# A residual load moved ahead of the FFN's operand loads, a q load moved to an earlier step, and a v store cut in four, in a fused attention and FFN kernel

## The chip, the cores and the metric

The kernel runs on one core of a Trainium2 chip. The metric is the time of one execution on the device in microseconds (us), the median of three runs.

## The reference

One prompt of S = 2048 tokens with D = 576 channels passes a block in three parts: a layer norm modulated by a condition c, an attention with a compressive memory, and a SwiGLU feed-forward network (FFN) with FF = 4608. Cut to what matters:

```
q, k, v = heads(h @ wq), heads(h @ wk), heads(h @ wv)   # 32 heads of 18, 4 segments of 512 tokens
phi = lambda t: where(t > 0, t + 1, exp(t))
for each segment:
    a_loc = softmax(q k^T * scale + mask) v
    a_mem = phi(q) M / (phi(q) z)
    a = sigmoid(beta) * a_mem + (1 - sigmoid(beta)) * a_loc
    M, z = M + phi(k)^T v, z + sum(phi(k))
x1 = x + gate_a * (a @ wo)                              # the residual
h2 = layernorm(x1), modulated
out = x1 + gate_b * ((silu(h2 @ w_gate) * (h2 @ w_up)) @ w_down)
```

h is the modulated layer norm of x. Everything is float32 in and out.

## The kernel before

The order of the instructions on each engine is the order in which the code emits them. Matrix products in float32 are made of parts: an operand is split into a rounded high half and a low half, and three or more matmuls take the place of one.

The span has four stages. Up to 230 us come layer norm and projections; `vproj` (line 593) makes v of one segment, and its results of segment 3 go from the SBUF tile `vs[3]` to `vD[3]` in device memory in one store by ScalarE's queue (line 608). From 230 to 578 us come the attention units, 32 of them: unit u is one segment and a group of heads. Each unit runs through 11 steps, and a table `PAT` (line 66) lists for each step the events that are woven into it; row 1 is that of the second and the fourth of a segment's eight groups. Event "f" loads phi(q)'s input `qF` for the next unit into the tile `qf` (`phi_q`, line 874), and ScalarE's `phi_q2` (events "g", lines 883 to 885) and PoolE's `phi_q3` ("h", line 892) work on it. `put_m` (line 195, line 198 in the trace) writes the maximum of the scores, `mr`, into the tile `qs`; "U" and "V" load k and q of a later unit. `wo_m` and `wo_x` (lines 823 and 837) are the output projection of the segment before: `wo_m` the matmuls, `wo_x` the sum with the residual input `xr` (line 840) and the store of the sum to `xD` (line 842). `load_xr` (line 799) loads `xr` from the input; each tile of 128 tokens of a segment has one, and the buffers are reused by the segment after.

From 578 to 597 us the output projection of segment 3 runs by itself, while the operands of the FFN's first block are loaded: `load_o` loads the tile `O` of gate and up weights (512 KB), `load_y` one of seven activation operands `y` (1024 + 192 KB), `load_r` small weight parts `wr`, `load_d` the down weights `dr`. From 597 us on comes the FFN: `step` (line 1348) runs one of seven products of a block by `prod` (line 1308, matmuls of line 1315). The first products run in the order 1, 6, 2, 7, 5, 4; product 2 takes y operand 1, product 7 operand 5, product 5 operand 3, and the operands of 6 and 4 (and 3) are made on the chip. ScalarE copies a product's bank (`cu`, `tb`, `tc`, line 1344) and casts weights to their high half `wh` (line 1276), VectorE makes the low half `wl` (line 1277) and sums of `O` (line 1265), PoolE other sums of `O` (line 1270) and of `dr` (lines 1291, 1298). `store_o` (line 1253) stores the sums of `O` to `oD` on ScalarE's queue.

Two more things set the order. DMAs go out on SyncE's and ScalarE's queues, each in order. Each DMA takes one of eight semaphores in turn, and its queue first waits until the last DMA with the same semaphore has landed. So a DMA can wait for a much earlier one of the other queue.

In the setup of the FFN (about line 1520), tiles 0 to 2 of `xr` of segment 3 are loaded first, and tile 3 only after `load_d`, because its buffer still holds segment 2's tile 3. That tile isn't stored by `wo_x` (the exception in line 841) but by a store right ahead of this load (line 1531).

Of the kernel before, what the change touches and what calls it, by code (L numbers as in the profile page):

```python
# [15 lines left out]
P = 128  # L16
S = 2048
D = 576
# [45 lines left out]
E2 = 1  # L64
BK = 0
PAT = (["E", "", "m U D", "c", "n V G", "Q d", "M0", "g M1 M2 M3 X", "h A0", "R S q T Y Z B0", "A1 f P z B1 C"],
# [3 lines left out]
LNA = 1  # L70
# [8 lines left out]
def f32(ap):  # L79
    return ap.bitcast(F32)  # L80
# [3 lines left out]
def block(ctx: ExitStack, tc: tile.TileContext, x, wqk, wv, wo, beta, wgu, wgr, wd, c, crow, w_mod, w_mod0, w_mod1, w_modc, xt, out):  # L84
    nc = tc.nc
# [7 lines left out]
    def chain(*g):  # L93
        for a in g:
            yield from a

    def once(g):
        yield next(g)
# [5 lines left out]
    def mm14(ps, wh, wl, xh, xl, xr, wstat):  # L104
        k = 0
        for kt in range(5):
            if kt < 4:
                pairs = [(wh(kt), xh(kt)), (wl(kt), xh(kt)), (wh(kt), xl(kt))]
            else:
                pairs = [(wh(4), xr()), (wl(4), xr())]  # L110
            for w, a in pairs:
                a, b = (w, a) if wstat else (a, w)
                nc.tensor.matmul(ps, lhsT=a, rhs=b, start=(k == 0), stop=(k == 13))  # L113
                k += 1
# [49 lines left out]
    vD = [dr.tile([P, 4, VC], F32, tag=f"vD{s}", name=f"vD{s}") for s in range(NSEG)]  # L164
# [3 lines left out]
    xD = [dr.tile([P, 4, D], F32, tag=f"xD{s}", name=f"xD{s}") for s in range(NSEG)]  # L168
# [105 lines left out]
    with ExitStack() as p1:  # L274
# [70 lines left out]
        with ExitStack() as p0:  # L345
# [41 lines left out]
            for b in range(3):  # L387
                n = P if b < 2 else 64
# [174 lines left out]
        def proj(s, t):  # L563
            hh, hl, hr = hT[s]
            pp = first.pop(t, None) if s == 0 else None
            if pp is None:
                pp = ps.tile([P, L], F32, tag="p", name="pp", bufs=3)
                mm14(pp, lambda k: wqkh[:, t, k, :], lambda k: wqkl[:, t, k, :], lambda k: hh[k],
                     lambda k: hl[k], lambda: hr, True)
            f = pb.tile([P, L], F32, tag="pf", name="pf")  # L570
            fb = pb.tile([P, 2, L], F32R, tag="fh", name="fh", bufs=3)
            fh, fl = fb[:, 0], fb[:, 1]
            if t < 5:
                nc.scalar.copy(f, pp)
            nc.scalar.copy(fh, pp)
            nc.vector.tensor_tensor(fl, pp, f32(fh), op=ALU.subtract)
            if s > 0 and t >= 5:
                nc.scalar.copy(f, pp)
            k0, k1 = 128 * t, min(128 * t + 128, D)
            if k0 < D:  # L580
                nc.sync.dma_start(kD[s][k0:k1], f32(fb[:k1 - k0]))
            q0, q1 = max(128 * t - D, 0), 128 * t + 128 - D
            if q1 > 0:
                r = P - q1 + q0
                nc.sync.dma_start(qD[s][q0:q1, 0:2], f32(fb[r:]))
                nc.sync.dma_start(qD[s][q0:q1, 2], f32(fh[r:]))
                if s > 0:
                    nc.sync.dma_start(qF[s][q0:q1, :], f[r:])
            return f

        vs = {}

        def vproj(s, i):
            hh, hl, hr = hT[s]
            if i == 0:
                vs[s] = w1.tile([P, 4, VC], F32, tag="vs", name=f"vs{s}", bufs=2)
                nc.gpsimd.memset(vs[s][:, :, :H * VW].rearrange("p i (a b) -> p i a b", b=VW)[:, :, :, DH:], 1.0)
                nc.gpsimd.memset(vs[s][:, :, H * VW:], 0.0)
            for h in range(2):
                pv = ps.tile([P, L], F32, tag="p", name="pv", bufs=3)  # L600
                sl = slice(288 * h, 288 * h + 288)
                tk = slice(128 * i, 128 * i + 128)
                mm14(pv[:, :288], lambda k: wvh[:, k, sl], lambda k: wvl[:, k, sl], lambda k: hh[k][:, tk],
                     lambda k: hl[k][:, tk], lambda: hr[:, tk], False)
                o = vs[s][:, i, 304 * h:304 * h + 304].rearrange("p (a b) -> p a b", b=VW)
                nc.scalar.copy(o[:, :, :DH], pv[:, :288].rearrange("p (a b) -> p a b", b=DH))
            if i == 3:
                nc.scalar.dma_start(vD[s], vs[s])

        for t in range(1, 4):  # L610
# [16 lines left out]
        for s in range(NSEG):  # L627
            if s == 0:
                gp, gw = prep(1), load_wv()
                g = chain(once(gp), once(gw), once(gp), once(gw), once(gp), gw, gp)  # L630
            else:
                g = prep(s + 1) if s + 1 < NSEG else iter(())
# [6 lines left out]
            for t in QKORD:  # L639
# [4 lines left out]
                f = proj(s, t)  # L644
# [13 lines left out]
            for i in range(4):  # L658
                if i == 3:
                    run(g)  # L660
                vproj(s, i)
                next(g, None)
                next(g, None)
                if s > 0:
                    for _ in range(E2):
                        next(ge, None)
                    next(gl, None)
# [117 lines left out]
    oT, orr, pto = {}, {}, {}  # L785
# [13 lines left out]
    def load_xr(s, i):  # L799
        xr = o3.tile([P, D], F32, tag="xr", name="xr") if s < 3 or i in (0, 3) else xp.tile([P, D], F32, tag="xs", name="xr")  # L800
        r = L * s + P * i
        nc.sync.dma_start(xr, x[r:r + P, :])
        return xr
# [33 lines left out]
    def wo_x(s, i, h):  # L837
        xr = oT[s, i][2]
        sl = slice(288 * h, 288 * h + 288)
        nc.vector.tensor_tensor(xr[:, sl], wps[0][:, :288], xr[:, sl], op=ALU.add)  # L840
        if h == 1 and (s, i) != (2, 3):
            nc.sync.dma_start(xD[s][:, i, :], xr)

    lnv = {}
# [389 lines left out]
    def load_y(t, o):  # L1234
        nc.sync.dma_start(f32(y[:, o, 0:4]), yD[t][o][:, 0:4])
        nc.sync.dma_start(f32(y[0:96, o, 4]), yD[t][o][0:96, 4])
# [8 lines left out]
    def load_o(t, p, z):  # L1245
        O[p, z] = o = opl.tile([P, 7, 2, P], F32, tag="O", name="O", bufs=2)
        if t == 0:
            nc.sync.dma_start(o[:, 0:4], wgu[p, z])
        else:
            nc.sync.dma_start(o[:, 0:3], wgu[p, z][:, 0:3])  # L1250
            nc.sync.dma_start(o[:, 3:7], oD[p][z])
# [4 lines left out]
    def load_r(p, z):  # L1256
        b, g = divmod(2 * p + z, 4)
        for i in range(3):
            nc.sync.dma_start(f32(R[z][32 * i:32 * i + 32]), rD[b][i % 2][32 * g:32 * g + 32])
# [20 lines left out]
    def load_d(t, p):  # L1280
        RW[p] = r = rp.tile([P, 7, 288], F32, tag="d", name="dr_")
        if t == 0:
            for f in range(2):
                nc.sync.dma_start(r[:, 2 * f:2 * f + 2].rearrange("p a b -> p (a b)"), wd[2 * p + f])
        else:
            nc.sync.dma_start(r[:, :NS[p]], wdD[p][:, :NS[p]])
# [157 lines left out]
    def plain(t, p, c):  # L1444
        pd = new_dn("pd", c)
        b, h, c = c // 4, c // 2 % 2, c % 2
        for i in range(2):
            tk = slice(128 * (2 * c + i), 128 * (2 * c + i) + 128)
            k = 0
            for f in range(2):  # L1450
                ah, al = AP[p % 2, (f, b)]
                dh, dl = DP[p % 2, (f, h)]
                for a, w in ((ah, dh), (ah, dl), (al, dh)):
                    nc.tensor.matmul(pd[:, i, :288], lhsT=a[:, tk], rhs=w, start=(k == 0), stop=(k == 5))  # L1454
                    k += 1
        d = x11[t] if b and h else acc[2 + h + 2 * b]
        o = d[:, 2 * c:2 * c + 2]
        nc.vector.tensor_tensor(o, o, pd[:, :, :288], op=ALU.add)
        if p == NPR - 1:
            if t:  # L1460
                store(t, b, h, d, c)
            elif c == 1:
                return lambda: store(t, b, h, d)
# [9 lines left out]
    with tc.manual_schedule():  # L1473
# [7 lines left out]
        for u in range(NU + 1):  # L1481
            s, q = divmod(u, 8)
# [35 lines left out]
        xr3 = {i: load_xr(3, i) for i in range(3)}  # L1518
# [5 lines left out]
        load_y(0, 0)  # L1524
        load_o(0, 0, 1)
        load_r(0, 0)
        load_y(0, 1)
        load_y(0, 5)
        load_y(0, 3)
        load_d(0, 0)  # L1530
        nc.sync.dma_start(xD[2][:, 3, :], oT[2, 3][2])
        xr3[3] = load_xr(3, 3)
        load_r(0, 1)
        wo_r(3, 0)
        wo_z(3)
# [9 lines left out]
        for i in range(4):  # L1545
            for h in range(2):
                for c in range(WC):
                    n = 8 * i + 4 * h + c
# [34 lines left out]
        n, nw = 0, PF  # L1583
# [5 lines left out]
        for t in range(2):  # L1589
            for p in range(NPR):  # L1590
# [18 lines left out]
                for k in range(14):  # L1609
                    z, m = ZM[k]  # L1610
# [59 lines left out]
                    if prev is not None and is_plain(*prev):  # L1670
# [3 lines left out]
                        if (CHE if t == 0 else CHB if p == 0 else CH0)[k]:  # L1674
                            f = plain(*prev, chunk)
# [123 lines left out]
```

## Time and profile before

| | us |
|---|---|
| median of 3 runs | 1837.87 (1834.95 to 1840.02) |
| profiled execution | 1840.8 |
| its span | 1839.0 |
| PE busy | 1797.0 |
| DVE busy | 1486.7 |
| ACT busy | 1086.2 |
| POOL busy | 675.4 |

PE is TensorE, DVE VectorE, ACT ScalarE, POOL GpSimd, SP SyncE; a q behind a name (SPq) is the engine's sequencer, which issues DMAs. Times are from the start of the span. Rows of the timeline give the start, the duration, engine, line, operation and tile (out<-in), and in brackets the idle time of the engine ahead of the instruction and what ended it. Rows of waits give who waited for whom, the total, the number of times and the longest. Rows of the chain give the pieces of the path that ends last. Rows of windows give the stretch, its length, the busy time and number of instructions of PE, weight load, DVE, ACT and POOL, the granted clock of TensorE, the busy share of the DMA engines and GB/s.

### The profile page before, as it was taken

What the parts mean: (1) busy time and instruction counts of PE and PEld (TensorE: products, weight loads), DVE (VectorE), ACT (ScalarE), POOL (GpSimd) and SP (SyncE); (2) the same over time, 40 slices, a digit from 0 to 9 for tenths busy, and PEclk for the clock granted to TensorE, in tenths of its full rate; (3) what the DMA queues carried; (4) which work ended last, traced back from release to release, by engine and by line L of the source; (5) the groups of instructions that cost most, each with busy time, mean ns of one, the idle gap of its engine ahead of it and who ended that gap; (6) DMA issues with size and microseconds to landing.
All of it is one profiled execution on the core that took longest, in us unless ns stands there. A gap on an engine that the chain in (4) does not pass through costs nothing.

```text
span 1839.0 us, 31444 instructions
## 1 busy us (share of the span) xinstructions
PE 1797.0 (98%) x10627; PEld 1525.5 (83%) x10627; DVE 1486.7 (81%) x3371; ACT 1086.2 (59%) x2371; POOL 675.4 (37%) x1104
## 2 busy tenths in 40 slices
PE   7999999999999799999999999999999999999999
PEld 5888866777777688888888888898888888888888
DVE  7556387888885599898889899868888888888886
ACT  4333287878776467777777777634454544544541
POOL 3444067775566375665665665400000000000000
PEclk9999999999999899999999999999999999999999
DMA  7768765667656745445555444484433333334331
GB/s 275 258 220 285 247 200 176 213 196 224 173 165 183 242 133 191 156 156 177 157 156 185 139 135 168 149 292 165 128 106 89 117 106 113 102 97 128 106 102 52
DMA packets 146003, 306.26 MB, mean 167 GB/s; under 512 B 30932, under 2 KB 61780, under 8 KB 143924
## 3 DMA queue, kind: packets, MB, share of 16 engines
q1 hardware_dynamic: 135092, 260.19, 45.7%
q10 hardware_dynamic: 10752, 44.07, 6.1%
q8 instruction: 85, 1.39, 0.3%
q14 instruction: 74, 0.61, 0.1%
HBM read 198.69 MB, written 104.94 MB: 165 GB/s over the span
## 4 chain that ended last, share of the span: by engine, by line
PE 91%; DMA 3%; ACT 2%; DVE 2%; issue 1%; SPq 1%; POOL 0%; ACTq 0%; DVEq 0%; POOLq 0%
PE A L1315 25%; PE pd L1434 19%; PE C L1315 13%; PE B L1315 6%; PE pp L113 6%; PE av L725 4%; PE s L210 4%; PE pv L113 3%; PE s L701 3%; PE pd L1454 3%; PE pw L835 3%; ACT Pt L708 1%; PE pn L903 1%; DMA xD<-xr 1%; DMA qf<-qF 1%
## 5 line engine op out<-in xcount | busy, mean ns | idle before, releaser
L1315 PE MATMUL A<-y,wh 128*128 128x512 f32 x1152 | 405.2, 392 | 11.8 <-ACT tb L1344 11.1
L1442 DVE TENSOR_TENSOR acc<-acc,pd 128x576 f32<-128x576 f32 x327 | 245.0, 750 | 79.2 <-PE pd L1434 73.1
L215 DVE CUSTOM_DVE_ANT_0 junk<-s,tri 128x256 bf16<-128x256 f32 (+3 forms) x512 | 221.4, 484 | 63.2 <-PE s L210 50.0
L1434 PE MATMUL pd<-dh,ah 128*128 128x288 f32 x896 | 267.3, 298 | 0.0
L1434 PE MATMUL pd<-dl,ah 128*128 128x288 f32 x896 | 263.7, 294 | 0.0
L1434 PE MATMUL pd<-dh,al 128*128 128x288 f32 x896 | 262.4, 293 | 0.0
L1315 PEld LDWEIGHTS A<-y,wh 128*128 128x128 f32 x1152 | 216.8, 188 | 51.0 <-ACT tb L1344 11.5
L1277 DVE TENSOR_TENSOR wl<-O,wh 128x256 fp32r<-128x256 f32 x504 | 238.8, 477 | 1.4 <-ACT wh L1276 0.7
L1315 PE MATMUL A<-y,wl 128*128 128x512 f32 x576 | 225.1, 391 | 0.0
L708 ACT ACTIVATE Pt<-s 128x512 f32<-128x512 f32 (+1 forms) x352 | 182.7, 558 | 46.0 <-PE s L701 28.9
L1276 ACT CAST wh<-O 128x256 fp32r<-128x256 f32 x504 | 198.3, 406 | 13.9 <-DVE xr L840 12.4
L1315 PE MATMUL C<-y,wh 128*128 128x512 f32 x576 | 203.4, 394 | 0.0
L1434 PEld LDWEIGHTS pd<-dh,ah 128*128 128x128 f32 x896 | 168.1, 188 | 18.7 <-ACT pd L1410 4.0
L1270 POOL TENSOR_TENSOR O<-O 128x128 f32<-128x128 f32 x280 | 155.0, 587 | 76.2 <-DMA O<-in_wgu_dram 35.0
L1434 PEld LDWEIGHTS pd<-dl,ah 128*128 128x128 f32 x896 | 169.5, 189 | 16.2
L1380 DVE TENSOR_TENSOR al<-sg,ah 128x512 fp32r<-128x512 f32 x240 | 176.6, 736 | 6.7 <-ACT ah L1379 6.5
L1434 PEld LDWEIGHTS pd<-dh,al 128*128 128x128 f32 x896 | 169.0, 189 | 0.0
L1379 ACT CAST ah<-sg 128x512 fp32r<-128x512 f32 x240 | 149.0, 621 | 24.3 <-DVE sg L1339 23.7
L701 PE MATMUL s<-qs,ks 110*128 110x512 f32 (+2 forms) x384 | 143.7, 392 | 6.8 <-ACT Pt L708 4.6
L210 PE MATMUL s<-ks,qs 108*128 108x256 f32 (+3 forms) x512 | 144.1, 335 | 2.6 <-DVE mx L215 2.2
L1315 PEld LDWEIGHTS C<-y,wh 128*128 128x128 f32 x576 | 108.6, 189 | 19.0
L1315 PEld LDWEIGHTS A<-y,wl 128*128 128x128 f32 x576 | 108.5, 188 | 14.9
(389 smaller groups left out, 4077.5 us busy)
## 6 DMA issues: line engine op xcount, KB each, us to landing
wr<-rD SPq DMA_DIRECT2D x216, 112.0 KB
O<-in_wgu_dram SPq DMA_DIRECT2D x36, 512.0 KB
oD<-O ACTq DMA_DIRECT2D x36, 512.0 KB
O<-oD SPq DMA_DIRECT2D x36, 512.0 KB
ks<-kD SPq DMA_DIRECT2D x96, 144.0 KB
O<-in_wgu_dram SPq DMA_DIRECT2D x36, 384.0 KB
qs<-qD SPq DMA_DIRECT2D x64, 192.0 KB
y<-yD SPq DMA_DIRECT2D x11, 1024.0 KB
```

Source lines behind the costliest of these rows:

```text
L113: nc.tensor.matmul(ps, lhsT=a, rhs=b, start=(k == 0), stop=(k == 13))
L210: nc.tensor.matmul(bank[:, n * (h - h0):n * (h - h0) + n], lhsT=qst[b][0:108, h, 128 * i:128 * i + 128], rhs=kst[b][0:108, h // 2, 0:n], s ...
L215: nc.vector.tensor_tensor_reduce(junk[:, :n], bank[:, n * (h - h0):n * (h - h0) + n], tri[:, L - n:], 1.0, -3e38, op0=ALU.add, op1=ALU.max ...
L701: nc.tensor.matmul(bank[:, n * (g - h):n * (g - h + w)].rearrange("p (a b) -> p a b", a=w), lhsT=kst[u % NB][0:110, g // 2, 128 * j:128 * ...
L708: nc.scalar.activation(pt[:, h:h + per, :n], bank[:, :n * per].rearrange("p (a b) -> p a b", a=per), AF.Exp, scale=SCALE)
L1270: eng.tensor_tensor(o[:, d, i, s_], o[:, a, i, s_], o[:, b, i, s_], op=op)
L1276: nc.scalar.copy(wh, o)
L1277: later.append(lambda: nc.vector.tensor_tensor(wl, o, f32(wh), op=ALU.subtract))
L1315: nc.tensor.matmul(bank, lhsT=a, rhs=b, start=(first and n == 0), stop=(n == 6), skip_group_check=not first)
L1380: later.append(lambda: nc.vector.tensor_tensor(al, src, f32(ah), op=ALU.subtract))
L1434: nc.tensor.matmul(pd[:, i, :288], lhsT=a[:, tk], rhs=w, start=(add and k == 0), stop=(k == 2), skip_group_check=not add)
L1442: nc.vector.tensor_tensor(o, o, pd[:, :, :288], op=ALU.add)
```

## The change

Four edits in three parts. The first part: `wo_x` stores every tile to `xD`, tile 3 of segment 2 too, and the load of segment 3's tile 3 stands right behind `load_r(0, 0)`, ahead of the y loads. The second: event "f" stands in step 1 of row 1 of the table and not in step 7, for six units. The third: in segment 3 each of four token tiles of v is stored by itself once it is made.

```
-       ["U E D", "", "Q l m", "", "M0 M1 M2 M3 X G p n V A0 B0", "", "A1 q c x B1", "f d", "", "", "C g Y h P"],
+       ["U E D", "f", "Q l m", "", "M0 M1 M2 M3 X G p n V A0 B0", "", "A1 q c x B1", "d", "", "", "C g Y h P"],
...
-            if i == 3:
+            if s == 3:
+                nc.scalar.dma_start(vD[s][:, i], vs[s][:, i])
+            elif i == 3:
                 nc.scalar.dma_start(vD[s], vs[s])
...
         nc.vector.tensor_tensor(xr[:, sl], wps[0][:, :288], xr[:, sl], op=ALU.add)
-        if h == 1 and (s, i) != (2, 3):
+        if h == 1:
             nc.sync.dma_start(xD[s][:, i, :], xr)
...
         load_r(0, 0)
+        xr3[3] = load_xr(3, 3)
         load_y(0, 1)
         load_y(0, 5)
         load_y(0, 3)
         load_d(0, 0)
-        nc.sync.dma_start(xD[2][:, 3, :], oT[2, 3][2])
-        xr3[3] = load_xr(3, 3)
         load_r(0, 1)
```

Lines behind the second edit are 2 higher in the kernel after (842 becomes 844), those behind the last 1 higher. The order of TensorE, VectorE and PoolE stays as it is.

SyncE's queue where attention ends, before (rows of DMAs, out<-in, with the shape; y<-yD_123 is operand 5, yD_121 operand 3):

```order
L1259 DMA wr<-rD_0_198 32x896
L1235 DMA y<-yD_119 128x2048
L1236 DMA y<-yD_119 96x512
L1235 DMA y<-yD_123 128x2048
L1236 DMA y<-yD_123 96x512
L1235 DMA y<-yD_121 128x2048
L1236 DMA y<-yD_121 96x512
L1284 DMA dr__8588<-in_wd_dram 128x576 x2
L1531 DMA xD_142<-xr 128x576
L802 DMA xr<-in_x_dram 128x576
L1259 DMA wr<-rD_0_198 32x896
```

The same stretch of SyncE's queue after the change:

```order
L1261 DMA wr<-rD_0_198 32x896
L804 DMA xr<-in_x_dram 128x576
L1237 DMA y<-yD_119 128x2048
L1238 DMA y<-yD_119 96x512
L1237 DMA y<-yD_123 128x2048
L1238 DMA y<-yD_123 96x512
L1237 DMA y<-yD_121 128x2048
L1238 DMA y<-yD_121 96x512
L1286 DMA dr__8594<-in_wd_dram 128x576 x2
L1261 DMA wr<-rD_0_198 32x896
```

The load passes seven DMAs; its store has left this stretch and stands some ten rows further up, behind the last store to `xh` and ahead of the loads of the three other `xr` tiles.

SyncE's queue in an odd unit, before (`mr` is the maximum of the scores):

```order
L187 DMA ks_80<-kD_106 36x2x512 x3
L198 DMA qs_87<-mr 1x16x128 x2
L193 DMA qs_79<-qD_102 48x2x512 x2
L193 DMA qs_79<-qD_102 6x2x512 x2
L1137 DMA rD_0_198<-yh_2509 128x896
L1138 DMA rD_1_199<-yh_2509 128x896
L1128 DMA yh_2509<-in_wgr_dram 128x512
L877 DMA qf<-qF_111 126x512
L992 DMA woraw<-in_wo_dram 128x576
```

The same after:

```order
L187 DMA ks_80<-kD_106 36x2x512 x3
L879 DMA qf<-qF_111 126x512
L198 DMA qs_87<-mr 1x16x128 x2
L193 DMA qs_79<-qD_102 48x2x512 x2
L193 DMA qs_79<-qD_102 6x2x512 x2
L1139 DMA rD_0_198<-yh_2512 128x896
L1140 DMA rD_1_199<-yh_2512 128x896
L1130 DMA yh_2512<-in_wgr_dram 128x512
L994 DMA woraw<-in_wo_dram 128x576
```

The load of `qf` passes the copies into `qs` and three DMAs of another job.

ScalarE at the end of `vproj` of segment 3, before:

```order
L606 COPY vs_2342<-pv 128x16x18 x3
L336 COPY gbB<-pc 128x288 x2
L606 COPY vs_2342<-pv 128x16x18 x4
L608 DMA vD_117<-vs_2342 128x2496
L708 ACTIVATE Pt<-s_2540 128x512
```

And after:

```order
L606 COPY vs_2342<-pv 128x16x18
L608 DMA vD_117<-vs_2342 128x624
L606 COPY vs_2342<-pv 128x16x18 x2
L608 DMA vD_117<-vs_2342 128x624
L336 COPY gbB<-pc 128x288 x2
L606 COPY vs_2342<-pv 128x16x18 x2
L608 DMA vD_117<-vs_2342 128x624
L606 COPY vs_2342<-pv 128x16x18 x2
L608 DMA vD_117<-vs_2342 128x624
L710 ACTIVATE Pt<-s_2543 128x512
```

Four quarter stores stand between the copies in place of one store behind the last.

More of the change, by code (lines that the diff above doesn't have):

```diff
@@ L606, in vproj @@
                 nc.scalar.copy(o[:, :, :DH], pv[:, :288].rearrange("p (a b) -> p a b", b=DH))
-            if i == 3:
+            if s == 3:
+                nc.scalar.dma_start(vD[s][:, i], vs[s][:, i])
+            elif i == 3:
                 nc.scalar.dma_start(vD[s], vs[s])
@@ L840, in wo_x @@
         nc.vector.tensor_tensor(xr[:, sl], wps[0][:, :288], xr[:, sl], op=ALU.add)
-        if h == 1 and (s, i) != (2, 3):
+        if h == 1:
             nc.sync.dma_start(xD[s][:, i, :], xr)
@@ L1526, in block @@
         load_r(0, 0)
+        xr3[3] = load_xr(3, 3)
         load_y(0, 1)
@@ L1530, in block @@
         load_d(0, 0)
-        nc.sync.dma_start(xD[2][:, 3, :], oT[2, 3][2])
-        xr3[3] = load_xr(3, 3)
         load_r(0, 1)
```

2 rows, old and new, of the table PAT are left out of this document.

## The prediction

> **What bounds the kernel now.** I read the summed chain first, then the chain piece by piece round the point where attention ends, then the engines' own rows there.
>
> ```profile
> PE 91%; DMA 3%; ACT 2%; DVE 2%; issue 1%; SPq 1%; POOL 0%; ACTq 0%; DVEq 0%; POOLq 0%
> ```
>
> TensorE carries 91% of the chain, so an edit that leaves its work alone can win only where it idles on the chain. The 3% of DMA is mostly in one place:
>
> ```profile
> 571.80 0.45 DVE xr L840
> ...
> 590.05 3.74 PE pw L835 x28
> ...
> 593.81 0.46 DVE xr L840
> 594.27 0.22 DVE O L1265
> 594.49 11.22 DMA xD<-xr
> ...
> 605.73 3.37 DMA xr<-in_x_dram
> ...
> 609.22 0.46 DVE xr L840
> ...
> 611.66 0.38 DVE xr L840
> ...
> 612.06 0.40 ACT wh L1276
> ...
> 614.35 3.35 PE A L1315 x7
> ```
>
> Last on the chain are a 288 KB store of a residual tile of segment 2, which takes 11.22 us, and the load into the same buffer, 3.37 us. VectorE stands at the sum that needs this load (line 840, tile 3 of segment 3), ScalarE behind VectorE, TensorE behind ScalarE. TensorE's rows, with the idle time before an instruction in brackets:
>
> ```profile
> 601.48 0.39 PE L1315 MATMUL B<-y,wh 128*128 128x512 f32 x1
> ...
> 602.84 0.39 PE L1315 MATMUL B<-y,wr 128*128 128x512 f32 x1
> 614.35 0.79 PE L1315 MATMUL A<-y,wh 128*128 128x512 f32 x1 [11.12 <-ACT tb L1344]
> 614.94 0.63 PE L1315 MATMUL A<-y,wl 128*128 128x512 f32 x1
> ...
> 620.05 0.40 PE L1315 MATMUL A<-y,wh 128*128 128x512 f32 x1
> ```
>
> Six steps from 601.48 to 602.84 are 0.227 us a matmul. Without the wait product 7 would begin at 602.84 + 0.23 = 603.07, product 5 seven matmuls later at 604.66, product 4 at 606.25. Product 4 began at 620.05. So the wait costs **13.8 us**: 11.1 of idling and 2.5 to 2.7 of slow matmuls after it (14 take 5.70 us where 3.18 would do). The windows (busy us of each engine, then granted clock, share of the DMA engines, GB/s) show the same:
>
> ```profile
> 560.00:580.00 20.00, 16.85 (x140) 12.10 (x141) 7.68 (x18) 13.15 (x29) 10.77 (x17) 1.00 0.39 124
> 580.00:600.00 20.00, 19.32 (x143) 18.61 (x142) 12.40 (x23) 9.09 (x19) 13.89 (x18) 1.00 1.00 286
> 600.00:610.00 10.00, 3.23 (x14) 2.31 (x13) 0.78 (x3) 0.00 (x0) 5.59 (x13) 0.79 0.68 203
> 610.00:615.00 5.00, 0.65 (x2) 0.56 (x3) 4.94 (x12) 2.92 (x8) 1.04 (x2) 0.50 1.05 404
> 615.00:620.00 5.00, 5.00 (x14) 3.94 (x13) 1.34 (x3) 3.03 (x5) 1.39 (x4) 0.55 0.94 292
> 620.00:640.00 20.00, 20.00 (x97) 16.92 (x97) 16.52 (x31) 11.80 (x29) 8.14 (x15) 1.00 0.57 192
> ```
>
> The clock is 0.50 to 0.55 after the idle stretch and 1.00 from 620, with TensorE full: time won ahead of 620 is kept. The Trainium skill ("TensorE: Matmul & The Clock Gate", What's actually happening) says that an idle window of about 3.4 us halves the clock and about 3.4 us of work restores it; by that rule a wait that shrinks below it costs its idling alone, and the rows here agree, with 0.63 us a matmul at 614.94 against 0.40 at 620.05.
>
> **The change part by part.** *Store and load of the residual tile.* SyncE's rows (start, then issue time with its blocking):
>
> ```profile
> 574.07 1.35 SPq L802 DMA_DIRECT2D xr<-in_x_dram  x3
> ...
> 579.16 2.59 SPq L1259 DMA_DIRECT2D wr<-rD  x3
> 581.79 0.55 SPq L1235 DMA_DIRECT2D y<-yD  x1
> ...
> 589.92 0.34 SPq L1235 DMA_DIRECT2D y<-yD  x1
> ...
> 613.50 0.33 SPq L1248 DMA_DIRECT2D O<-in_wgu_dram  x1
> ```
>
> The store's data is ready at 571.80 + 0.45 = 572.25, so in the new place SyncE issues it at about 574.0, while the queue is nearly empty (124 GB/s was the mean of the 20 us before 580); it lands long before the load is issued behind the three wr loads, at 579.16 + 2.59 plus the store's 0.35, about **582.2**. What was issued from 574.1 to 581.8 (three xr loads, two of O, a y operand of 1.2 MB, wr) is 3.4 MB, 12 us at the window's 286 GB/s, so until 588 from about 576 on; with the store and the load itself, 0.59 MB or 2.1 us more, and a us to land, it is there at about **591**, with 588 and 593 as bounds (0.9 MB less or 0.6 MB more). VectorE needs it when TensorE ends the first half of tile 3: 28 matmuls of the two halves of tile 2 end at 593.8, the next half takes half of their 3.74, so 595.7. Margin 2.7 to 7.7 us.
>
> VectorE then runs what it ran from 609.22 to 611.66, which is 2.44, and reaches the second half's sum at 598.1; from 611.66 to 614.35 were 2.69, so product 7 could begin at 600.8. But ScalarE has this ahead of it:
>
> ```profile
> 599.12 0.59 ACT L1344 COPY cu<-A 128x512 f32<-128x512 f32 x1 [5.58 <-PE A L1315]
> 609.18 2.84 ACTq L1254 DMA_DIRECT2D oD<-O  x2
> ```
>
> From the copy's end at 599.7, two issues (0.35 to 0.5 each), then 614.35 - 612.06 = 2.29 of casts and the copy tb: 602.9, as TensorE arrives at 603.07. This wait is gone by a hair.
>
> Next late are the operands. The moved store and load are 0.59 MB that now pass before the y loads instead of behind them: 0.59 / 0.286 = **2.1 us** for everything behind. Of the y loads the last is nearest to its use (the rows are PoolE's, and one of ScalarE for the next paragraph):
>
> ```profile
> 604.41 3.60 POOL L1291 TENSOR_TENSOR dr__8588<-dr__8588,gbB 128x144 f32<-128x144 f32 x8 [9.91 <-DMA dr__8588<-in_wd_dram]
> ...
> 618.61 3.74 POOL L1270 TENSOR_TENSOR O<-O 128x128 f32<-128x128 f32 x8 [7.57 <-DMA O<-in_wgu_dram]
> ...
> 624.59 0.41 ACT L1276 CAST wh<-O 128x256 fp32r<-128x256 f32 x1
> ```
>
> The first wd load landed at 604.4; y for product 5 stands right ahead of it, so it landed 0.29 MB, or 1 us, earlier at the latest, and 2 us at the earliest: 602.4 to 603.4. Plus 2.1: 604.5 to 605.5, against 604.66 for its use. Stall 0 to 0.9 from this alone. The two oD stores of ScalarE (1.05 MB) were issued at 609.18, just behind the landed load, and now at about 600, beside these loads. Where they ran beside SyncE's before, the DMA moved 404 GB/s (610 to 615), against 286 without; so they take little from the others: with the same ratio the 1.05 MB cost between 0 and 1 us. I take **+1.0** for product 5, bounds 0 and 4.5. The Trainium skill ("DMA: Bandwidth & Descriptors", Issuing engines are not separate DMA queues) says that DMAs of several engines interleave on the same 16 DMA engines and that only issue time is saved. By it the stores would push y by up to 1.05 / 0.286 = 3.7 us; the 404 GB/s speak against the full price, and that is a rival below.
>
> Then the second O load, of the next hidden block. It was issued at 613.50, landed at 618.61, and its last use was not pressed: ScalarE took it up at 624.59. In the new order everything on TensorE is up to 13.8 us earlier, so its use comes near 611; but SyncE reaches it only after the wr loads, the four xD stores (which wait for VectorE's sums, now from 596 to 599, not 609 to 612) and the landing of the second wd load at 604.4 + 1 + 2.1 = 607.5. Issue at 608.3, landing after the 5.1 us that it took before: **613.4**, bounds 612 and 616. That is 2.5 us behind its use; PoolE's 3.74 of sums and ScalarE's casts then run late, while TensorE has some products prepared. I take **+1.5** on TensorE, bounds 0 and 4.
>
> *Part "f"* (row 1 of the table, step 7 to step 1; six loads of 252 KB):
>
> ```profile
> ACT qe L883 <- DMA qf<-qF: 2.8, 3, 1.7
> ...
> 256.98 0.47 PE L701 MATMUL s<-qs,ks 110*128 110x512 f32 x1 [2.13 <-ACT woh L998]
> ...
> 278.03 0.68 PE L701 MATMUL s<-qs,ks 110*128 110x256 f32 x2 [1.85 <-ACT Pt L708]
> ```
>
> ScalarE's wait for the load goes, 2.8 us in three places; two of them are followed by the only TensorE idlings of note in the attention stage, 2.13 and 1.85. They can fall by no more than the waits, 2.8 in sum; PoolE's chain behind (its mask and its sums, the rows run on without gaps) keeps a part. In its new place the load stands ahead of SyncE's copy of the maximum (qs from mr), and waits there for PoolE to have read the old tile: a cost of 0.3 of issue, up to 1 us of blocking at each of six places. I take **-1.5**, bounds -2.8 and +1.
>
> *Part v* adds three DMA issues on ScalarE at gaps, and cuts the last store from 1248 to 312 KB:
>
> ```profile
> SPq L193 <- DMA vD<-vs: 7.9, 1, 7.9
> ...
> 237.00 0.50 PE L701 MATMUL s<-qs,ks 110*128 110x512 f32 x1 [1.00 <-ACT Pt L708]
> ...
> 228.52 0.40 ACT L606 COPY vs<-pv 128x288 f32<-128x288 f32 x1 [1.46 <-PE pv L113]
> 230.37 0.40 ACT L606 COPY vs<-pv 128x288 f32<-128x288 f32 x1 [1.45 <-PE pv L113]
> 230.80 0.33 ACTq L608 DMA_DIRECT2D vD<-vs  x1
> ```
>
> ScalarE idles 1.45 us ahead of each copy, which hides an issue of 0.33; uncovered the three would cost 1.0. SyncE waited 7.9 us for the store, but the one idling of TensorE over 0.7 us between 231 and 256 is the 1.00 at 237.0, and that is ScalarE's. **0**, bounds -0.5 and +0.5.
>
> The sum: -13.8 + 1.0 + 1.5 - 1.5 + 0 = **-12.8 us**, against the profiled execution's 1840.8 (span 1839.0): 1828.0. That execution is 2.9 above the median of 1837.87; I take the difference over to the median: **1825.1**.
>
> **The rivals.** *(a) All of it, nothing late behind it*: the queue drains as with 404 GB/s and both late terms are 0: -15.3, **1822.6**. For it: margins of 0 to 1 us only have to fall right. Against: the use near 611 of a load issued at 608.
>
> *(b) Crowding*: by the sharing rule y for product 5 is 3.7 later, so TensorE stalls some 4.5 us, past the length after which the clock fell; 1.5 of slow matmuls follow, O adds 2.5 more. -13.8 + 4.5 + 1.5 + 2.5 - 1 = -6.3: **1831.6**. For it: DMA share 1.00 from 580 to 600.
>
> *(c) The change does not do what it says*: the load is still behind something (its issue waits for an earlier DMA on its semaphore, or the store waits in the backlog) and lands past 608. Then -1.5 from "f" and nothing more, **1836.4**. Against: all DMAs ahead of it were issued by 581.8.
>
> *(d) Slower*: the second O load becomes the bound. SyncE must wait, ahead of it, for the landing of both oD stores and of the wd load. The loss equals the whole gain when O lands 15.3 us after its use near 611, at 626 and later; each us beyond is a us slower. At 630: **1842**. Against: in the old order it landed at 618.61 with all its predecessors held until 605.73; now they are issued 6 to 23 us earlier.
>
> **How the numbers follow.** Forecast 0.47, (a) 0.25, (b) 0.18, (c) 0.06, (d) 0.04. Range: from (a) with all of "f", 1821, to (b), 1832; this leaves out (c) and (d). A difference of 0.3%, 5.5 us, is about what a measurement of this kernel can tell from no change. Faster by more (under 1832.4): forecast, (a) and most of (b), 0.88. Within: (c) and the rest of (b), 0.08. Slower: (d), 0.04.
>
> **What would show it.** Right: SyncE issues the xD store near 574 and the xr load near 582; VectorE's sum of tile 3 waits for TensorE, not for a DMA; product 7 begins at 603 to 604, its matmuls at 0.39 us, and the windows show clock 1.00 from 600 to 620. The late terms show as an idle before product 5 with a DMA or nothing named, and a PoolE wait for O at 611 to 614. "f" shows as 256.98's and 278.03's idling gone. Wrong: an idle of over 3.4 us before product 7 or 5, clock 0.5 again, or the chain running through the second O load.

## The result, and the profile after

| | us |
|---|---|
| before, median of 10 runs | 1838.35 (1834.48 to 1841.9) |
| after, median of 10 runs | 1832.7 (1829.19 to 1836.05) |
| ratio | 0.997, 95% interval 0.9958 to 0.9982 |
| span of the profiled execution, before and after | 1839.0 and 1831.1 |

The change makes the kernel 5.6 us faster (3.3 to 7.7 by the interval). The forecast was 12.8 us. The long wait ahead of product 7 is gone, and less than half of its price came back. The two profiled executions, whose rows follow, differ by more, 7.9 us (1840.8 and 1832.9): that of the kernel before was some 2.4 us above the median of its runs, that of the kernel after at it.

TensorE's rows after (the instructions that stood at 614.35, 617.50, 620.05, 621.65 and 637.55 before stand at 602.76, 606.58, 608.75, 611.49 and 630.34):

```profile
593.22 0.37 PE L837 MATMUL pw<-woh,oh 128*128 128x288 f32 x1 [0.87 <-ACT y L1152]
...
602.53 0.39 PE L1317 MATMUL B<-y,wr 128*128 128x512 f32 x1
602.76 0.39 PE L1317 MATMUL A<-y,wh 128*128 128x512 f32 x1
...
606.58 0.50 PE L1317 MATMUL C<-y,wh 128*128 128x512 f32 x1 [2.08 <-DMA y<-yD]
...
608.75 0.63 PE L1317 MATMUL A<-y,wh 128*128 128x512 f32 x1
...
611.49 0.40 PE L1317 MATMUL A<-y,wh 128*128 128x512 f32 x1
...
630.34 0.51 PE L1317 MATMUL A<-y,wh 128*128 128x512 f32 x1 [1.56 <-ACT B L1363]
```

The last two of these before:

```profile
621.65 0.39 PE L1315 MATMUL A<-y,wh 128*128 128x512 f32 x1
...
637.55 0.39 PE L1315 MATMUL A<-y,wh 128*128 128x512 f32 x1
```

Product 7 follows product 2 without a gap. Product 5 then waits 2.08 us for its y operand. So TensorE is 11.3 us ahead at product 4 (608.75 against 620.05), 10.2 at 611.49 (against 621.65), and only 7.2 at 630.34 (against 637.55); the span ends 7.9 ahead.

VectorE's residual sums show that the moved load is not what is late (in brackets what the sum waited for):

```profile
578.30 0.46 DVE L842 TENSOR_TENSOR xr<-pw,xr 128x288 f32<-128x288 f32 x1 [0.84 <-PE pw L837]
...
595.34 0.46 DVE L842 TENSOR_TENSOR xr<-pw,xr 128x288 f32<-128x288 f32 x1 [0.25 <-PE pw L837]
```

The sum at 595.34, of segment 3, waits for TensorE and not for a DMA. The one at 578.30 is the second half of segment 2's tile 3, whose store has moved. SyncE's rows after:

```profile
571.54 0.34 SPq L872 DMA_DIRECT2D xh<-xh  x1
578.78 0.34 SPq L844 DMA_DIRECT2D xD<-xr  x1
579.21 1.35 SPq L804 DMA_DIRECT2D xr<-in_x_dram  x3
580.66 0.38 SPq L1250 DMA_DIRECT2D O<-in_wgu_dram  x1
581.09 0.43 SPq L1237 DMA_DIRECT2D y<-yD  x1
...
585.42 0.43 SPq L804 DMA_DIRECT2D xr<-in_x_dram  x1
...
594.56 0.32 SPq L1237 DMA_DIRECT2D y<-yD  x1
```

SyncE stands from 571.9 to 578.8 at the store, until that sum has ended (578.30 + 0.46), and the three xr loads, O and y start behind it: 579.21, 580.66 and 581.09, against 574.07, 576.85 and 577.27 before. SyncE's rows of waits (570 to 612) put 6.8 us of the store's wait down to VectorE's sum of `xr` (line 842 there, 840 before). Five of these microseconds in the windows (the last two numbers are the DMA engines' busy share and GB/s), before and then after:

```profile
575.00:580.00 5.00, 4.29 (x49) 2.69 (x42) 0.89 (x3) 1.03 (x2) 2.01 (x4) 1.00 0.95 291
```

```profile
575.00:580.00 5.00, 4.29 (x38) 4.19 (x35) 1.97 (x5) 1.82 (x4) 2.46 (x3) 1.00 0.07 28
```

The DMA engines idle where they were full: 263 GB/s less in 5 us are 1.3 MB, which is one y operand with its tail. The chain after runs through what that delays, the wr and the last y load (issued at 594.56, once a wr load ahead of it has landed), and then TensorE:

```profile
584.91 9.64 DMA wr<-rD
...
594.56 11.97 DMA y<-yD
...
606.58 2.37 PE C L1317 x7
```

### The profile page after: what moved, and what is told of

Read it like the earlier page. It is cut to its first block, busy times and chain, and to the rows that moved or that the text cites. A ratio compares the mean times of both kernels' runs of the same rounds, so it can differ in the third digit from the quotient of the medians.

```text
span 1831.1 us, 31448 instructions
## 1 busy us (share of the span) xinstructions
PE 1794.8 (98%) x10627; PEld 1524.0 (83%) x10627; DVE 1489.0 (81%) x3371; ACT 1085.3 (59%) x2371; POOL 677.9 (37%) x1104
## 4 chain that ended last, share of the span: by engine, by line
PE 89%; DMA 4%; ACT 2%; POOL 2%; DVE 1%; SPq 1%; issue 1%; ACTq 0%; POOLq 0%; DVEq 0%
PE A L1317 25%; PE pd L1436 19%; PE C L1317 12%; PE B L1317 6%; PE pp L113 5%; PE av L727 4%; PE s L210 4%; PE pv L113 3%; PE s L703 3%; PE pd L1456 3%; PE pw L837 2%; ACT Pt L710 1%; PE pn L905 1%; PE pm L543 1%; DMA y<-yD 1%
```

## The experiments

The theory (blocking): the store of segment 2's tile 3 needs a sum that VectorE makes only near 580; SyncE's queue is in order, so everything behind the store waits with it while the DMA engines idle. The rival (bytes): 0.59 MB ahead of the y loads is all that delays them. Ratios are against the kernel before, with 95% intervals; 0.001 is 1.8 us. e1, e2, e4 and e5 ran on one chip, e3 and e6 to e8 on a second, e9 to e12 on a third, each beside the kernel before.

**e1, the residual part alone.** The first and the last hunk of the change, with "f" and v as before.

> Only the residual part: the store of segment 2's tile 3 in place and the early load; "f" and the v store as before. From the profiles, TensorE was 2.3 us ahead at 580 by the other parts and 7.9 ahead at the end, so the residual part should give about -5.5 us (-3.5 to -7.5) whatever the cause of its small size. My theory (blocking: SyncE stands at the store until VectorE's sum, near 580, and three xr loads, O and y wait behind it) expects the store's issue at 580 to 581 here, 2 us later than in the changed kernel as TensorE is 2 us later, the DMA near idle from 576 to 580, and an idle of TensorE before product 5 of 1.5 to 3 us. The rival (bytes: 0.59 MB moved ahead of y is all that delays y) expects the same time, but no idle stretch of the DMA that matters.

Measured: 1835.4 against 1838.23, ratio 0.9988 (0.998 to 0.9997), so -2.2 us (-0.5 to -3.7): below what was expected. SyncE issued the store at 578.23, not at 580 to 581, since TensorE was as early here without "f" as it was with it (that stage varies from one execution to the next, below). The idle stretch (windows under e10) and the wait are there:

```profile
602.14 0.47 PE L1315 MATMUL A<-y,wh 128*128 128x512 f32 x1 [0.47 <-DMA y<-yD]
...
606.38 0.80 PE L1315 MATMUL C<-y,wh 128*128 128x512 f32 x1 [2.40 <-DMA y<-yD]
```

**e2, "f" alone.**

```
-       ["U E D", "", "Q l m", ..., "f d", "", "", "C g Y h P"],
+       ["U E D", "f", "Q l m", ..., "d", "", "", "C g Y h P"],
```

> Only "f" in step 1. If the profile of the changed kernel is right, the idlings of TensorE at 257 and 278 go and about 2 us are new at 280 (product of memory and phi(q) behind PoolE): -2 to -3.5 us, kept to the end, because the handover to the FFN starts earlier but waits for the same late load; if that load's time is set by the DMA queue and not by TensorE, the gain is lost there and the time is that of before, 0 to -1.

Measured: 1835.78 against 1838.23, ratio 0.9986 (0.9977 to 0.9996): -2.6 us (-0.7 to -4.2). It is kept to the end.

**e3, the v store in four parts alone.**

```
-            if i == 3:
+            if s == 3:
+                nc.scalar.dma_start(vD[s][:, i], vs[s][:, i])
+            elif i == 3:
```

> Only the v store in four parts. Nothing on TensorE waited for it before: 0, -0.5 to +0.5 us against before. A rival (SyncE's 7.9 us of blocking held q loads that TensorE missed in most executions): -1 to -3 us.

Measured: 1839.32 against 1837.94, ratio 1.001 (1.0 to 1.002). No gain; a loss of 0 to 3.7 us is at the edge of what can be told. e9 and e12 below bear on it again.

**e4, the store behind the first y operand.** The whole change, with the condition on (2, 3) kept in `wo_x` and the store emitted later:

```
         load_y(0, 0)
+        nc.sync.dma_start(xD[2][:, 3, :], oT[2, 3][2])
         load_o(0, 0, 1)
         load_r(0, 0)
         xr3[3] = load_xr(3, 3)
```

> The whole change, but the store of segment 2's tile 3 is issued behind the first y operand's loads and not ahead of the three xr loads. The bytes ahead of y operands 1, 5 and 3 are the same as in the changed kernel. Blocking theory: SyncE finds the sum ready, the loads behind run some 4 us earlier, product 5 waits at most 0.5 us, and 2 to 4 us of the 5 that were lost come back: 2 to 4 us faster than the changed kernel, -8 to -10 against before. Bytes theory: within 1 us of the changed kernel, -5 to -6.5. A third: SyncE now stands at the load of tile 3 until the store behind the backlog has landed (near 586), and y is as late as before: also -5 to -6, but with the wait at the load.

Measured: 1827.17 against 1838.23, ratio 0.9945 (0.9933 to 0.9957), -10.1 us. The bytes ahead of the y loads are those of the changed kernel, so the bytes theory falls here. SyncE did not find the sum ready, as the theory had expected: it still stands 2.7 us at the store. The wait at the load that the third case names is there too (the load was issued at 584.11):

```profile
SPq L804 <- DMA xD<-xr: 3.3, 1, 3.3
...
SPq L1527 <- DVE xr L842: 2.7, 1, 2.7
```

But O and the first y operand had gone out ahead of both waits: from 575 to 580 the DMA moved 372 GB/s where the changed kernel moved 28. And y was not late: product 5 begins at 602.34, seven matmuls behind product 7 at 600.75.

**e5, a buffer of its own for the load.** Segment 3's tile 3 gets one more buffer, and the store goes behind the down weights' loads, as before.

```
-        xr = o3.tile([P, D], F32, tag="xr", name="xr") if s < 3 or i in (0, 3) else ...
+        xr = o3.tile([P, D], F32, tag="xr", name="xr") if s < 3 or i == 0 else o3.tile([P, D], F32, tag="xq", name="xr", bufs=1) if i == 3 else ...
...
         load_d(0, 0)
+        nc.sync.dma_start(xD[2][:, 3, :], oT[2, 3][2])
         load_r(0, 1)
```

> The whole change, but segment 3's tile 3 has a buffer of its own: its load stands where the change put it and waits for no store, and segment 2's tile 3 is stored behind the down weights' loads, as before. Blocking theory: SyncE stands nowhere for the sum, 0.29 MB less is ahead of y, product 7 and product 5 begin without a wait and TensorE isn't held at 590: -11 to -13 us against before, less what the second O load still costs (2 to 4): -8 to -11. Bytes theory: 0.29 MB is 1 us less delay, so -6 to -7.

Measured: 1826.35 against 1838.23, ratio 0.9945 (0.9933 to 0.9958): -10.1 us, as e4.

**e6, the store in place alone.** The kernel before, with every store in `wo_x`, and the load where it was.

```
-        if h == 1 and (s, i) != (2, 3):
+        if h == 1:
...
-        nc.sync.dma_start(xD[2][:, 3, :], oT[2, 3][2])
         xr3[3] = load_xr(3, 3)
```

> Of the residual part only the store in place; segment 3's tile 3 is loaded where it was before, behind the down weights' loads; "f" and v as before. The load no longer waits for a store right ahead of it, which took 11.22 + 3.37 us; issued at 594.5 it would land about where the store landed, 605.7, 3.4 us earlier than before. Blocking theory: SyncE stands 4 to 5 us at the store, all the loads behind are that much later, and the 3.4 us are eaten: 0, -1.5 to +1.5 us against before. If the blocking costs nothing: -3 to -4.

Measured: 1842.69 against 1837.94, ratio 1.0028 (1.0018 to 1.0037): **5.1 us slower** (3.3 to 6.8), although the wait of the load for the store is gone. The sign is the theory's, the size beyond it. SyncE's rows and TensorE's product 7:

```profile
573.15 0.34 SPq L870 DMA_DIRECT2D xh<-xh  x1
580.39 0.34 SPq L842 DMA_DIRECT2D xD<-xr  x1
580.82 1.35 SPq L802 DMA_DIRECT2D xr<-in_x_dram  x3
...
599.28 0.33 SPq L802 DMA_DIRECT2D xr<-in_x_dram  x1
```

```profile
616.41 0.80 PE L1315 MATMUL A<-y,wh 128*128 128x512 f32 x1 [11.78 <-ACT tb L1344]
```

SyncE stands 6.9 us at the store; the load that was issued at 605.73 before goes out at 599.28, 6.5 us earlier, and yet product 7 begins 2 us later than before. The queue ahead of the load is later: PoolE's work on the wd load right ahead of it begins at 608.85 and not at 604.41, and VectorE's sum that needs the load itself at 610.73 and not at 609.22. This profile accounts for these 2 us; where the rest of the 5.1 is lost isn't shown (the profiled execution of before was itself above its median).

**e7, both buffers, the store in place.** As e5, but with the store where the change has it.

> The whole change with a buffer of its own for segment 3's tile 3, but the store of segment 2's tile 3 stays in place, where SyncE stands for the sum. It differs from e5 in the store's place alone, and from the changed kernel in the buffer alone. Blocking theory: as the changed kernel, -4.5 to -6.5 us against before. If it was the load's wait for the store, and not the store's wait for the sum, that cost the gain: as e5, -10 to -11.

Measured: 1832.17 against 1837.94, ratio 0.9968 (0.9955 to 0.998): -5.9 us, the changed kernel's. From e5 it differs in the store's place alone; that is worth 4.2 us by the ratios, though the two intervals just overlap, and the buffer nothing that can be measured.

**e8, e4 and e5 together.** Store as in e4, buffer as in e5.

> e4 and e5 together: the store behind the first y operand's loads, and the load in a buffer of its own. In e4 SyncE stood 3.3 us at the load until the store had landed; here it stands at neither. If that wait still costs (TensorE: all y earlier, the second O load too): -11 to -13 us. If the DMA queue had work enough behind it, so that the wait is hidden: as e4, -10 to -11.

Measured: 1828.47 against 1837.94, ratio 0.9946 (0.9932 to 0.996): -9.9 us. The load's wait for the store was hidden in e4. From e7, on the same chip, it differs in the store's place alone: 4.0 us, the same price again.

**e9, e4 without the v part.**

> e4 (the whole change with the store behind the first y operand) without the v part: v is stored once, as before. By e3, v alone took +1.8 us (0 to +3.7). If that is v's: -11.5 to -13 us against before, 1 to 2 us below e4. If e3's figure was chance or came from a place that e4 has not: as e4, -9 to -11.

Measured: 1827.53 against 1838.47, ratio 0.9936 (0.9924 to 0.9949): -11.8 us. That is 1.7 us below e4, the way e3 points, but the intervals overlap.

**e10, the residual part alone with the store behind.** As e4, with "f" and v as before.

> The residual part alone, with the store behind the first y operand; "f" and v as before. With the store in place the residual part alone gave -2.2 us (-0.5 to -3.7). Blocking theory: the store's place is worth 5 us and the part gives -7 to -9. If the parts are not additive (e4's gain rests on "f" having brought TensorE ahead): -3 to -6.

Measured: 1830.92 against 1838.47, ratio 0.9953 (0.994 to 0.9965): -8.6 us, where e1 gave -2.2. The store's place decides over **6.4 us** in this part; the two intervals do not touch. The windows, e1 and then e10:

```profile
570.00:580.00 10.00, 8.65 (x75) 6.02 (x75) 3.34 (x9) 5.19 (x11) 5.59 (x7) 1.00 0.19 64
```

```profile
570.00:580.00 10.00, 8.65 (x75) 5.98 (x74) 2.68 (x8) 4.65 (x10) 4.67 (x8) 1.00 0.65 220
```

The DMA moves 220 GB/s in these 10 us against 64, 1.6 MB more. In e10 product 5 begins seven matmuls behind product 7, with no wait, product 4 comes at 605.42, 14.6 us earlier than before, and the later place (637.55 before) at 626.22, 11.3 earlier:

```profile
602.25 0.39 PE L1315 MATMUL A<-y,wh 128*128 128x512 f32 x1
...
603.84 0.39 PE L1315 MATMUL C<-y,wh 128*128 128x512 f32 x1
...
605.42 0.39 PE L1315 MATMUL A<-y,wh 128*128 128x512 f32 x1
...
626.22 0.53 PE L1315 MATMUL A<-y,wh 128*128 128x512 f32 x1 [1.61 <-ACT B L1361]
```

**e11, sums moved from PoolE to VectorE.** e4, and in the first block:

```
-                            sum_o(nx, 1, 2 * k - 20)
-                            sum_o(nx, 1, 2 * k - 19)
+                            sum_o(nx, 1, 2 * k - 20, nc.vector if dl else nc.gpsimd)
+                            sum_o(nx, 1, 2 * k - 19, nc.vector if dl else nc.gpsimd)
```

> e4, and in the first block the four sums of the second hidden block's other half of gate and up weights are VectorE's and not PoolE's. In e4 TensorE loses 2 to 3 us from 612 to 625 against the profile before; ScalarE waited there for PoolE, whose rows are full from 611 to 622. If PoolE's chain behind the late second O load is what costs it: 1 to 2.5 us below e4. If the landing of the load itself or ScalarE's stores behind it cost it: as e4, within 1 us.

Measured: 1826.67 against 1838.47, ratio 0.9929 (0.9916 to 0.9942): -13.0 us, 2.9 below e4 by the ratios, though the intervals overlap. PoolE's rows in e10, which has these sums as e4 has them, and then in e11:

```profile
612.47 4.27 POOL L1270 TENSOR_TENSOR O<-O 128x128 f32<-128x128 f32 x8 [2.72 <-issue]
617.71 2.85 POOL L1270 TENSOR_TENSOR O<-O 128x128 f32<-128x128 f32 x4 [0.98 <-DMA O<-in_wgu_dram]
620.53 1.12 POOL L1298 TENSOR_TENSOR dr__8591<-dr__8591 128x144 f32<-128x144 f32 x2
621.61 1.94 POOL L1270 TENSOR_TENSOR O<-O 128x128 f32<-128x128 f32 x4
```

```profile
611.91 3.85 POOL L1272 TENSOR_TENSOR O<-O 128x128 f32<-128x128 f32 x8 [2.96 <-DMA O<-in_wgu_dram]
615.72 0.94 POOL L1300 TENSOR_TENSOR dr__8594<-dr__8594 128x144 f32<-128x144 f32 x2
```

The landing of O is the same, 612 in both; PoolE is done at 616.7 and not at 623.6. TensorE's busy time (the first number behind the length) in the 37 us from 603 on, e10 and then e11:

```profile
603.00:640.00 37.00, 34.40 (x166) 28.37 (x165) 28.93 (x50) 19.51 (x45) 25.03 (x45) 1.00 0.69 235
```

```profile
603.00:640.00 37.00, 36.14 (x175) 29.62 (x174) 30.72 (x55) 20.71 (x48) 21.73 (x40) 1.00 0.65 218
```

It is 1.7 us fuller. The wait of 1.61 us for ScalarE's copy B at 626.22 in e10 stands in e4 and e9 too (1.8 and 1.6), and in e11 and e12 it is gone. So the chain of sums on PoolE behind the late second O load is at least a part of what TensorE loses there.

**e12, e9 and e11 together.**

> e9 and e11 together. If both are right, -13 to -15 us against before; if v is nothing and PoolE's chain is nothing, as e4, -10.

Measured: 1825.72 against 1838.47, ratio 0.9929 (0.9917 to 0.9942): -13.0 us. e11, which differs from it by the v part alone, has the same ratio. So e12 shows no price of v where e3, and e9 against e4, point to a loss of 1.7 to 1.8 us; a small loss is neither shown nor ruled out. From e9, on the same chip, e12 differs by the moved sums alone: 1.3 us by the ratios, with overlapping intervals, where e11 against e4 gave 2.9. The times alone do not tell the gain of the sums from nothing; the rows under e11 do.

## Why the prediction was wrong, point by point

**The bound.** Right: the wait of 11.1 us and the slow matmuls behind it are gone, and product 7 begins when TensorE comes to it (602.76; 603 to 604 was said).

**"The store's data is ready at 571.80 + 0.45 = 572.25."** This step failed, and the size of the forecast with it. The chain's row at 571.80 is the sum of the first half of tile 3. The store needs both halves. The second was in the trace of before, 8.6 us later, in VectorE's rows:

```profile
571.80 0.46 DVE L840 TENSOR_TENSOR xr<-pw,xr 128x288 f32<-128x288 f32 x1 [3.07 <-PE pw L835]
580.38 0.46 DVE L840 TENSOR_TENSOR xr<-pw,xr 128x288 f32<-128x288 f32 x1 [0.84 <-PE pw L835]
```

With 580.8 in place of 572.25 the store would have been seen to hold SyncE for nearly 7 us, from 574.0 on (in e6 and in the changed kernel it stood 6.9), with the three xr loads, O and y behind it. The sign that SyncE issues the store near 574 failed with it: it came at 578.78. The rivals named crowding, the second O load and a store that waits in the backlog, not a wait for the sum. e1 against e10 price it at 6.4 us in the residual part, and e7 against e5 at 4.2 us in the whole change; in e6 the store in its new place, with the load where it was, makes the kernel 5.1 us slower.

**The load lands in time.** Right in the changed kernel, although it was issued at 585.42 and not at 582.2. But the margin of 2.7 to 7.7 us was not there: in e1, with the same order, the sum waited 0.60 us for the load and began at 594.44.

**Operand for product 5, +1.0.** Too small: from 602.76 to 608.75 are 5.99 us, where 14 matmuls at full clock take 3.18, so 2.8 were lost to the wait of 2.08 and to the half clock behind it, and 1.2 more by 611.49. These 4.0 lie within the bounds of 0 to 4.5, but come from SyncE's standing: in e10 the same distance (602.25 to 605.42) takes 3.17. So the bytes, and the stores of oD beside them, were not the cause.

**Second O load, +1.5.** Too small too. From 611.49 on the changed kernel loses 10.2 - 7.2 = 3.0 us, and e10 from product 4 on 14.6 - 11.3 = 3.3. The prices are alike, but the late transfer behind them is not the same. In e10 it is the one that was named: ScalarE waits 2.21 us for O until 612.42, and PoolE begins its sums of O at 612.47, within the 611 to 614 that was said. In the changed kernel the down weights are late too (PoolE's work on them begins at 609.70, 604.41 before), and PoolE comes to the sums of O only behind it, without a gap:

```profile
609.70 4.46 POOL L1293 TENSOR_TENSOR dr__8594<-dr__8594,gbB 128x144 f32<-128x144 f32 x8 [14.52 <-DMA dr__8594<-in_wd_dram]
...
617.06 4.18 POOL L1272 TENSOR_TENSOR O<-O 128x128 f32<-128x128 f32 x8
```

There ScalarE waits 2.90 us for the sums of `dr`, until 617.13. With the store behind the first y operand, e11 shows PoolE's sums as a part of the price; for the changed kernel itself no run separates the two loads.

**A term that was missing.** TensorE was 2.1 us ahead at the sum of 578.30 (580.38 before) and 0.3 ahead at product 6 (599.45 against 599.76): 1.8 us lost in the last output projection, where it waits 0.42 at 588.40 and 0.87 at 593.22 for ScalarE. ScalarE had waited for O (2.06, until 587.02) and for PoolE's sums of O (1.96, until 590.22): the late O, one stage earlier. In e10 nothing is lost there (0.8 ahead at both places).

**"f", -1.5.** Measured -2.6 by itself (e2), more than forecast and inside the bounds. That PoolE's chain keeps a part is borne out: the wait of 2.13 us is gone, but at 278 the changed kernel waits for PoolE's pq.

```profile
278.43 0.45 PE L905 MATMUL pn<-mbd,pq 72*128 72x76 f32 x2 [2.05 <-POOL pq L894]
```

The upper bound of 2.8 was argued wrongly: it counted ScalarE's waits for the load, and not the clock that falls behind TensorE's idling (below).

**v, 0.** Not settled: e12 against e11 shows nothing, while e3 alone, and e4 against e9, point to a loss of 1.7 to 1.8 us, above the bound of 0.5 but at the edge of what can be told.

**From the profiled execution to the median.** The forecast took the 12.8 us over to the median unchanged, although the profiled execution of before was 2.9 us above it. The profiled executions differ by 7.9 us and the medians by 5.6, so 2.3 of the 7.2 us that are missing come in at this step. Where that execution lost them isn't shown.

**The rivals.** The time came out near (b), 1831.6, by another mechanism than (b) names; that its figure fits is chance.

## What to carry to other kernels

A DMA that is moved up in an in-order queue takes its data's due time with it: look up when the last of the instructions that write the data ends (count the halves of a tile), and what the queue issues behind it. A store whose data comes late belongs behind the loads that could go, even if that makes its buffer free later; e4, with the store six DMAs further down, has nearly twice the gain of the change. And when one long wait goes, look at the engine that the next late transfer feeds: here PoolE's sums, which VectorE had time for.

## What the runs showed of the hardware that was not expected

A short idle stretch of TensorE costs clock too. The granted clock after the wait of 2.08 us in the changed kernel (last three numbers: clock, DMA share, GB/s):

```profile
606.00:607.50 1.50, 0.92 (x4) 0.79 (x5) 0.00 (x0) 0.00 (x0) 0.00 (x0) 1.00 1.03 414
607.50:609.00 1.50, 1.50 (x6) 1.12 (x5) 0.00 (x0) 0.00 (x0) 0.00 (x0) 0.59 0.94 300
609.00:611.00 2.00, 2.00 (x6) 1.51 (x6) 1.66 (x3) 0.63 (x1) 1.30 (x2) 0.50 0.69 240
611.00:613.00 2.00, 2.00 (x10) 1.65 (x9) 0.39 (x1) 1.20 (x3) 2.00 (x6) 0.95 1.05 381
```

And in the kernel before, behind the wait of 2.13 us at 256.98:

```profile
256.00:258.00 2.00, 1.02 (x9) 0.38 (x12) 1.06 (x1) 2.00 (x6) 2.00 (x4) 0.93 0.85 191
258.00:260.00 2.00, 2.00 (x16) 0.61 (x12) 1.30 (x9) 0.83 (x2) 1.92 (x4) 0.50 0.31 53
```

About 3.4 us at half clock follow each, which is up to 1.7 us of TensorE's work, nearly the price of the wait once more. Behind the waits of 1.56 and 1.61 us (630.34 after, 626.22 in e10) the clock stayed at 1.00. Length alone doesn't decide: it stayed at 1.00 behind 1.84 us in e5 (614.18) and was 0.50 behind 1.85 us in the kernel before (278.03). The prediction took from the Trainium skill ("TensorE: Matmul & The Clock Gate", What's actually happening) that an idle window of about 3.4 us is needed, and priced shorter waits at their idling; the rows of 2.08 and 2.13 us disagree, and the measurement decides. That the clock came back after about 3.4 us of work agrees with the rows shown, but not with all: behind the 11.12 us it took some 5 us (614.35 to about 619.5), and behind the 1.85 us at 278.03 every window from 278.6 to 285.0 has 0.50.

Executions differ in the attention stage: e1 has "f" as before and yet waits there for 1.07 and 2.08 us where the profile before has 2.13 and 1.85. One profile can't price an edit of 2 us there.
